# A fused attention, routed experts and dense-layer kernel: a separate one-hot chain for the first expert block, other store queue, one more block in float32r parts, new planner priorities

## The chip, the cores and the metric

One NeuronCore of one Trainium2 chip runs the whole kernel in one launch. The metric is the device time in microseconds; below 0.3% of it two versions can't be told apart.

## The reference

Three layers follow one another. All inputs are float32, except the two dense weights, which are float64.

```
attention   q, k, v [2, 8, 768, 64]; each query sees 4 sink keys and its last 128 keys; softmax; a @ v
            -> x [1536 tokens, 512]
experts     do_compute = x @ w_skip > 0;  logits = x @ w_gate (8 experts);  e = argmax, g = softmax(logits)[e]
            x += g * (relu(x @ w1[e]) @ w2[e])   for tokens with do_compute;  w1 [8, 512, 1024], w2 [8, 1024, 512]
dense       h = x @ w_in [512, 2048];  g = h if h > 0 else exp(h) - 1;  out = g @ w_out [2048, 512]
```

## The kernel before

**Order.** Nothing is scheduled by hand. A planner, the class `Plan` at the head of the file, takes a list of steps (`add`), each with the engines that can do it, an estimated time, the steps it follows, the buffers it needs and a priority. It simulates the five instruction queues ("e" TensorE, "d" VectorE, "a" ScalarE, "p" GpSimd, "s" SyncE). It starts at each point the step of lowest priority number among those that can start within a small margin. The order that comes out is what each engine's queue holds, so a step that the planner put too early makes its engine wait. The table `ADJ` shifts priorities, for a whole kind of step (key -1) or one tile of it, in units of a tile; its entries "a", "d", "e", "p", "s" are the margins.

**Attention**, 12 tiles of 128 tokens with 8 heads each: loads of k, q and v (`lk`, `lq`, `lv`, SyncE's queue; k and q share four buffers), transposes of k and q (`tk`, `tq`), scores (`qk`), mask and exp, transposes of the weights (`tp`), products with v (`av`), the output copied out of PSUM (`eo`), transposed back together with the gate columns (`tx`), scaled into rows (`fx`) and gate parts (`fm`), logits summed (`lm`). The rows go to a table in DRAM (`st`). While this runs, SyncE also loads weights of the first experts.

**Gate**, in groups of 4, 4, 2 and 2 tiles (`gate`): maximum, one-hot of the winning expert, rank within its expert by triangular and all-ones matmuls (`rk`), product of rank and one-hot (`t8`), the token's slot, and a table of token lists (`tab`, line 688). The gate weights go to DRAM by line 701.

**First expert block.** Its input is put together in PSUM. The rows of tiles 0 to 9 come by an early gather (line 862), which needs group 2's list. They are transposed (`bx00`). Tiles 10 and 11 add their own rows by a matmul with a one-hot of the slot (`hot0`, line 876; `own`, line 881). Then ScalarE or VectorE copies the sum out (`bxe`) and the first layer starts (line 915).

**Experts.** One block of 128 tokens per expert, and a ninth block for one list that overflows: gather (line 898), transpose, layer 1 (32 products), relu, layer 2, scatter. The gather of a block follows the one before it in the planner; the first waits for all stores. Blocks in `RB` split relu's output and w2 into a rounded float32r part (`hi`, line 938) and its remainder (`lo`) and multiply in three passes; the others multiply in float32. SyncE keeps loading weights.

**Dense layers.** Float64 weights are loaded as pairs of integers, turned into float32 by integer steps on VectorE (`cv`) and split in two parts. 48 steps (three groups of 512 tokens, 16 column chunks) then run layer 1 (line 1125), elu on ScalarE and VectorE (lines 1139 to 1150), layer 2 (line 1163). The conversions of the first group's chunks run beside it.

Of the kernel before, what the change touches and what calls it, by code (L numbers as in the profile page):

```python
# [17 lines left out]
P = 128  # L18
# [23 lines left out]
    "gqm": {1: 3.1},
    "hot0": {0: 0.3, 1: 2.5},
    "lk": {-1: -1.7, 3: -0.7, 8: 1.4, 9: 1.3, 10: 0.7, 11: -0.6},
    "lq": {-1: -1.3, 6: 1.3, 9: -0.2, 10: 1.1, 11: -0.9},
    "mask": {-1: -1.2},
    "mask1": {-1: 2.3},
    "p": {-1: 16.756},
    "qk": {-1: -4.3},
    "s": {-1: 0.06},  # L50
    "spt": {-1: -1.8, 2: 1.2, 4: 3.9, 10: -2.1},
# [7 lines left out]
class Plan:  # L59
# [25 lines left out]
    def run(self, adj={}, until=None):  # L85
# [90 lines left out]
def fused_kernel(  # L176
# [35 lines left out]
    NFILL = 6  # L212
# [13 lines left out]
    RB = (1, 2, 3, 4, 5, 8)  # L226
# [53 lines left out]
    gid0 = C([P, 1], I32, "gid0")  # L280
    hot0 = [C([P, P], F32, f"hot0{i}") for i in range(GROUPS[-1])]
# [215 lines left out]
    def attention(t):  # L497
# [67 lines left out]
        for g in range(2):  # L565
            def av(e, g=g):
# [15 lines left out]
                p0 + 0.1 * g + 0.09, need=[] if g else [("O", ("o", t), 1)],  # L582
# [10 lines left out]
        evict(("eo", t), lambda: sl(oT_t, ("oT", t)), lambda: bk(("o", t)), 512, [("av", t, 1)], p0 + 0.23, [("o", t)],  # L593
              need=[("oT", ("oT", t), 2)])
# [5 lines left out]
        for g in range(2):  # L600
# [5 lines left out]
            add(("tx", t, g), {"e": 0.5}, rows, [("eo", t), "eg"], p0 + 0.24, need=[("T", ("tx", t, g), 2)], use=[("oT", t)])  # L606
# [11 lines left out]
        add(("st", t), {"s": 0.45}, lambda e: nc.sync.dma_start(out=xtab[1 + t * P:1 + (t + 1) * P, 0:DM], in_=sl(x_t_, ("x", t))), [("fx", t, 1)], p0 - 2.6,  # L618
# [15 lines left out]
    def gate(gi):  # L634
# [10 lines left out]
        p0 = t0 + n - 1 + 0.28  # L645
# [55 lines left out]
        G("st", {"s": 0.45}, lambda e: nc.sync.dma_start(out=xtab[1 + t0 * P:1 + (t0 + n) * P, DM:DG].rearrange("(g p) o -> p g o", p=P),  # L701
# [68 lines left out]
    for i in range(6):  # L770
        def fill(e, i=i):
            nc.tensor.matmul(bk(("fill", i))[:, 0:256], ones, ones.rearrange("p (o n) -> p o n", o=1).to_broadcast([P, 2, P]), start=True, stop=True)
        if i < NFILL:
            add(("fill", i), {"e": 0.12}, fill, [("av", NTILE - 1, 1)] + ([("fill", i - 1)] if i else []), 1000.0, need=[("S", ("fill", i), 1)], use=[("fill", i)])
# [77 lines left out]
    def first_block():  # L852
# [18 lines left out]
        add("bx00", {"e": 0.44}, gathered, ["early", ("av", NTILE - 1, 1)], 11.25, need=[("S", ("bx", 0), 1)])  # L871
        for i in range(nl):
            t = t0 + i

            def hot(e, i=i):
                nc.vector.scalar_tensor_tensor(out=hot0[i], in0=iota, scalar=g8["t"][:, i, 0:1], in1=goh[:, i, 0:1].to_broadcast([P, P]), op0=ALU.is_equal, op1=ALU.mult)
            add(("hot0", i), {"d": 0.26}, hot, [("g", gl, "t8")], 11.2)
# [14 lines left out]
    def block(e):  # L892
# [9 lines left out]
        add(("gather", e), {"p": 1.1}, gather, ["aend", ("ov", 8) if last else "gidx"] + ([("gather", e - 1)] if e else stores), p0 - 25, lat=3.2,  # L902
# [652 lines left out]
```

## Time and profile before

| | |
|---|---|
| time, median of 3 runs | 531.11 us (529.7 to 531.55) |
| profiled execution | 530.91 us |
| span of its instructions | 529.1 us |
| busy: TensorE, VectorE, ScalarE, GpSimd | 506.6 (96%), 345.3 (65%), 203.6 (38%), 33.4 us |
| attention ends, first expert layer starts | 117.9, 126.8 us |
| dense layers start, last matmul ends | 255.8, 521.8 us |

Times in the rows are microseconds from the start of the span. An engine carries out its queue in order; the bracket behind a row gives its idle time and the instruction that ended it. DVE is VectorE, ACT ScalarE, POOL GpSimd, PE TensorE, SPq SyncE's queue. A float32 product stands as two matmul records.

### The profile page before, as it was taken

Reading aid. Unit: us, or ns where it says so; the run is one execution under the profiler, and the core shown is the slowest. Engines: PE = TensorE matmul, PEld = TensorE weight load, DVE = VectorE, ACT = ScalarE, POOL = GpSimd, SP = SyncE. Lnnn points to the kernel's source line nnn. Section 1 sums busy time; section 2 is a strip of 40 time slices with the busy share of each in tenths; the row PEclk is TensorE's granted clock in tenths of the full one; section 3 lists DMA queues with packets and bytes.
Section 4 is the critical chain, followed back from the end, with each engine's and each line's share of the span. In section 5 each row is a group of like instructions: output and inputs, shape, how many; then the busy total and the mean of one; then the engine's idle time right before and its main releaser. Section 6 shows DMA issues by size and latency. Waiting matters only on the chain.

```text
span 529.1 us, 8427 instructions
## 1 busy us (share of the span) xinstructions
PE 506.6 (96%) x3143; PEld 418.8 (79%) x3143; DVE 345.3 (65%) x874; ACT 203.6 (38%) x455; POOL 33.4 (6%) x47
## 2 busy tenths in 40 slices
PE   8989898997899999999999999999999999999994
PEld 4778786886599999779788888888888888888883
DVE  6867786878356686798999998463444545544342
ACT  3876766763033434353566664220101112001010
POOL 2000000001212111000000000100000010000000
PEclk9999999999999999999999999999999999999998
DMA  9999999418999699467555330220000002000002
GB/s 169 274 243 317 276 294 331 118 42 284 397 347 363 233 328 312 144 196 241 160 180 158 121 120 1 79 81 0 1 0 1 0 2 79 1 0 1 0 0 86
DMA packets 73155, 79.11 MB, mean 150 GB/s; under 512 B 43089, under 2 KB 51537, under 8 KB 73106
## 3 DMA queue, kind: packets, MB, share of 16 engines
q1 hardware_dynamic: 69826, 73.29, 44.9%
q0 software_dynamic: 1520, 4.99, 2.7%
q8 instruction: 26, 0.43, 0.3%
q10 hardware_dynamic: 1760, 0.22, 0.3%
q14 instruction: 23, 0.19, 0.1%
HBM read 69.82 MB, written 8.66 MB: 148 GB/s over the span
## 4 chain that ended last, share of the span: by engine, by line
PE 88%; DMA 7%; DVE 2%; issue 1%; ACT 1%; POOL 0%; DVEq 0%; ACTq 0%
PE bank L1125 25%; PE bank L1163 25%; PE bank L915 11%; PE bank L948 6%; DMA pl<-in_k_dram 4%; PE bank L574 4%; PE bank L533 4%; PE bank L951 3%; PE bank L462 3%; PE bank L605 2%; PE bank L561 2%; PE bank L579 1%; PE bank L560 1%; DMA r<-xtab,gidx 1%; DMA pl<-xtab,gid 1%
## 5 line engine op out<-in xcount | busy, mean ns | idle before, releaser
L1163 PE MATMUL bank<-m,gt 128*128 128x512 f32 x576 | 139.2, 390 | 0.0
L1163 PEld LDWEIGHTS bank<-m,gt 128*128 128x128 f32 x576 | 107.8, 188 | 22.2
L1125 PE MATMUL bank<-xTa,m 128*128 128x512 f32 x384 | 97.9, 390 | 0.6 <-DVE xTa L1067 0.6
L1143 ACT ACTIVATE re<-re 128x512 f32<-128x512 f32 x48 | 30.3, 632 | 156.7 <-DVE re L1141 156.3
L1125 PEld LDWEIGHTS bank<-xTa,m 128*128 128x128 f32 x384 | 72.0, 188 | 16.3 <-DVE xTa L1067 0.9
L1141 DVE TENSOR_SCALAR re<-bank 128x512 f32<-128x512 f32 x35 | 24.2, 692 | 74.9 <-PE bank L1125 74.9
L915 PEld LDWEIGHTS bank<-blk,pl 128*128 128x128 f32 x480 | 55.2, 192 | 2.5 <-issue 1.4
L915 PE MATMUL bank<-blk,pl 128*128 128x128 f32 x480 | 56.1, 275 | 0.7 <-ACT blk L347 0.7
L547 ACT ACTIVATE pw<-sm,rm 128x272 f32<-128x272 f32 (+2 forms) x96 | 47.1, 495 | 7.0 <-DVE rm L539 7.0
L1146 DVE SCALAR_TENSOR_TENSOR re<-re,bank 128x512 f32<-128x512 f32 x48 | 32.9, 686 | 23.9 <-ACT re L1143 23.7
L1125 PE MATMUL bank<-xTxb,m 128*128 128x512 f32 x144 | 40.4, 389 | 0.0
L539 DVE CUSTOM_DVE_ANT_0 sm<-bank,mk 128x272 f32<-128x272 f32 (+2 forms) x96 | 35.3, 407 | 6.0 <-PE bank L533 3.6
L948 PE MATMUL bank<-hl,hr 128*128 128x512 f32 (+1 forms) x168 | 36.3, 367 | 1.1 <-DVE delta L1051 1.1
L948 PEld LDWEIGHTS bank<-hl,hr 128*128 128x128 f32 x168 | 27.7, 189 | 5.5 <-DVE delta L1051 1.3
L1125 PEld LDWEIGHTS bank<-xTxb,m 128*128 128x128 f32 x144 | 27.0, 188 | 5.6
L292 DVE TENSOR_TENSOR gt<-re,gt 128x512 fp32r<-128x512 f32 x44 | 30.4, 690 | 1.0
L533 PE MATMUL bank<-kt,pl 64*128 64x272 f32 (+2 forms) x192 | 27.4, 407 | 0.0
L292 DVE TENSOR_TENSOR hl<-pl,hl 128x1024 fp32r<-128x1024 f32 x20 | 23.9, 1219 | 3.2 <-ACT hl L938 3.2
L347 ACT COPY PT<-bank 128x512 f32<-128x512 f32 (+1 forms) x40 | 20.6, 550 | 13.3 <-PE bank L561 11.0
L574 PE MATMUL bank<-PT,pl 128*64 128x128 f32 x352 | 24.5, 279 | 0.1
L1005 ACT ACTIVATE r<-raw 128x512 f32<-128x512 f32 x32 | 21.4, 677 | 8.0 <-DVE m L292 7.5
L574 PEld LDWEIGHTS bank<-PT,pl 128*64 128x64 f32 x352 | 18.7, 136 | 5.6 <-issue 2.8
(203 smaller groups left out, 653.8 us busy)
## 6 DMA issues: line engine op xcount, KB each, us to landing
pl<-in_moe_w_dram SPq DMA_DIRECT2D x62, 512.0 KB, 6.1
raw<-in_moe_w_in_dram SPq DMA_DIRECT2D x16, 512.0 KB, 4.1
raw<-in_moe_w_out_dram SPq DMA_DIRECT2D x16, 512.0 KB, 4.3
pl<-in_k_dram SPq DMA_DIRECT2D x12, 256.0 KB, 5.5
pl<-in_q_dram SPq DMA_DIRECT2D x12, 256.0 KB, 5.3
pl<-in_v_dram SPq DMA_DIRECT2D x12, 256.0 KB, 6.0
xtab<-pl SPq DMA_DIRECT2D x12, 256.0 KB, 5.1
out_dram<-raw SPq DMA_DIRECT2D x5, 512.0 KB, 3.0
```

Of the source, the lines that this page charges most:

```text
L292: CE[e].tensor_tensor(out=o, in0=a, in1=b, op=ALU.subtract)
L533: nc.tensor.matmul(o, qT[r, p, :], rhs, start=True, stop=True)
L539: nc.vector.tensor_tensor_reduce(out=sl(sm_t, ("sm", t, h))[:, 0:n], in0=bk(("s", t, h))[:, 0:n], in1=m, scale=-scale, scalar=3.0e38, op0= ...
L547: nc.scalar.activation(out=sl(pw_t, ("pw", t))[:, h, 0:n], in_=sl(sm_t, ("sm", t, h))[:, 0:n], func=ACTF.Exp, bias=rm[:, t, h:h + 1], scal ...
L574: nc.tensor.matmul(o[i * D:(i + 1) * D, p, :], vt[:, h * D:(h + 1) * D], pT[:, (0 if y else c - 2) + i, :], start=(p == 0 and (y == 1 or n ...
L915: nc.tensor.matmul(o[:, i, :], w_tile(("w", e, kk))[:, f * P:(f + 1) * P], sl(post["xT"], ("xT", e))[:, kk, :], start=(i == 0 and kk == 0) ...
L948: nc.tensor.matmul(y, h[:, a, f % 4, :], w[:, b], start=(f == 0 and j == 0), stop=(f == KF - 1 and j == 2))
L1125: nc.tensor.matmul(bk(name), w[:, a, kk, :], x[:, b], start=(kk == 0 and i == 0), stop=(kk == KD - 1 and i == 2))
L1141: nc.vector.tensor_scalar(out=r, in0=pt, scalar1=-1.0, scalar2=0.0, op0=ALU.mult, op1=ALU.max)
L1143: nc.scalar.activation(out=r, in_=r, func=ACTF.Exp, scale=-1.0)
L1146: nc.vector.scalar_tensor_tensor(out=r, in0=r, scalar=-1.0, in1=pt, op0=ALU.add, op1=ALU.max)
L1163: nc.tensor.matmul(bk(("acc", g, i)), gt[:, a, i * P:(i + 1) * P], w[:, b, :], start=(c == 0 and j == 0), stop=(c == NCH - 1 and j == 2))
```

## The change

- The planner credits 0.25 us to a TensorE step that follows a TensorE step, and `ADJ` has new values throughout.
- Ten more filler matmuls (16 for 6), of lowest priority, after the last attention matmul.
- For the first block, tiles 10 and 11 get their one-hot of expert 0 by a chain of their own, per tile: max over the logits, skip flag, column, rank by matmuls with a column, one-hot of the slot. The last tile's output copy is done in two halves, and the group before the last has a 0.6 lower priority number.
- The row stores of tiles 10 and 11 and the last gate-weight store are issued by ScalarE instead of SyncE.
- A gather no longer follows the gather before it but all stores; block 0's own gather has a later priority.
- Block 0's first layer is split in four steps. Block 6 is added to `RB`.
- Rounded copies (`hi`, step 5 of `cv`, and in the first token group steps 0 and 3 of elu) run on ScalarE alone; `hi` of block 1 waits for the index conversion.

```diff
 ADJ:  -    "qk": {-1: -4.3},   "lk": {-1: -1.7, ...},  "lq": {-1: -1.3, ...},  "p": {-1: 16.756},
       +    "qk": {-1: -20.5, ...},  "lk": {-1: -2.6, ...},  "lq": {0: -8.3, 1: -1.4, 2: -1.1},  "lv": {-1: -2.3, ...},  "p": {-1: 1.721},
...
-            o["at"] = max([self.by[a]["end"] for a in o["after"]], default=0.0)
+            o["at"] = max([self.by[a]["end"] - 0.25 * ("e" in o["eng"] and "e" in self.by[a]["eng"]) for a in o["after"]], default=0.0)
...
-    NFILL = 6
+    NFILL = 16
-    RB = (1, 2, 3, 4, 5, 8)
+    RB = (1, 2, 3, 4, 5, 6, 8)
...
+        halves_o = 2 if t == NTILE - 1 else 1
+        for i in range(halves_o):
+            w = 512 // halves_o
+            evict(("eo", t, i), lambda i=i, w=w: sl(oT_t, ("oT", t))[:, i * w:(i + 1) * w], lambda i=i, w=w: bk(("o", t))[:, i * w:(i + 1) * w], w, ...
...
-        add(("st", t), {"s": 0.45}, lambda e: nc.sync.dma_start(...
+        add(("st", t), {"a": 0.6} if last_t(t) else {"s": 0.45}, lambda e: (nc.scalar if last_t(t) else nc.sync).dma_start(...
...
-        p0 = t0 + n - 1 + 0.28
+        p0 = t0 + n - 1 + 0.28 - (0.6 if gi == len(GROUPS) - 2 else 0)
...
-        G("st", {"s": 0.45}, lambda e: nc.sync.dma_start(...
+        G("st", {"a": 0.6} if final else {"s": 0.45}, lambda e: (nc.scalar if final else nc.sync).dma_start(...
...
-        add("bx00", {"e": 0.44}, gathered, ["early", ("av", NTILE - 1, 1)], 11.25, ...
+        add("bx00", {"e": 0.44}, gathered, ["early", ("qk", NTILE - 1, 1)], 11.25, ...
...
-                nc.vector.scalar_tensor_tensor(out=hot0[i], in0=iota, scalar=g8["t"][:, i, 0:1], in1=goh[:, i, 0:1].to_broadcast([P, P]), op0=ALU.is_equal, op1=ALU.mult)
-            add(("hot0", i), {"d": 0.26}, hot, [("g", gl, "t8")], 11.2)
+            add(("f0", t), {"d": 0.24}, lambda e, i=i, lg=lg: V.tensor_reduce(out=gs0[i][:, 0:1], in_=lg(0, E), axis=AX.X, op=ALU.max), [("lm", t)], q)
+            add(("f1", t), {"d": 0.22}, lambda e, i=i, lg=lg: V.tensor_scalar(out=gs0[i][:, 1:2], in0=lg(E, E + 1), scalar1=0.0, scalar2=None, op0=ALU.is_gt), [("lm", t)], q)
+            add(("f2", t), {"d": 0.22}, lambda e, i=i, lg=lg: V.scalar_tensor_tensor(out=go0[i], in0=lg(0, 1), scalar=gs0[i][:, 0:1], in1=gs0[i][:, 1:2], op0=ALU.is_ge, op1=ALU.mult), ...
+            def rank0(e, i=i, t=t):
+                o = bk(("f3", t))[:, 0:1]
+                nc.tensor.matmul(o, ones, ohsum[:, 0:1], start=True, stop=False)
+                for x in range(i):
+                    nc.tensor.matmul(o, ones, go0[x], start=False, stop=False)
+                nc.tensor.matmul(o, utri, go0[i], start=False, stop=True)
+                nc.vector.scalar_tensor_tensor(out=hot0[i], in0=iota, scalar=bk(("f3", t))[:, 0:1], in1=go0[i].to_broadcast([P, P]), op0=ALU.is_equal, op1=ALU.mult)
...
-        ... + ([("gather", e - 1)] if e else stores), p0 - 25, lat=3.2,
+        ... + stores, (p0 if e else 36.0) - 25, lat=3.2,
...
+            if not e:
+                for h in range(2):
+                    add(("b1", e, n) if h else ("b1x", n), {"e": 1.78}, lambda eng, n=n, h=h: layer1(eng, n, (2 * h, 2 * h + 1)), ...
...
-                    add(("hi", e, i), {"a": 1.02, "d": 0.66}, ..., [("w", e, KD + i)], ...
+                    add(("hi", e, i), {"a": 1.02}, ..., [("w", e, KD + i)] + (["gidx"] if e == 1 else [("hi", e - 1 if e < 8 else 6, i)]), ...
-            add(nm(5), {"a": 0.63, "d": 0.40}, ...
+            add(nm(5), {"a": 0.63}, ...
-        add(L(0), {"a": 0.58, "d": 0.68}, ...
+        add(L(0), {"a": 0.58} if not g else {"a": 0.58, "d": 0.68}, ...
-        add(L(3), {"d": 0.37, "a": 0.63}, ...
+        add(L(3), {"a": 0.63} if not g else {"d": 0.37, "a": 0.63}, ...
```

## Rows read from the trace of the kernel before

**Rows 1.** Stages: start:end, us, busy PE, PEld, DVE, ACT, POOL; clock, DMA, GB/s

```profile
8.40:117.90 109.50, 104.46 (x1055) 84.67 (x1056) 82.42 (x393) 78.39 (x260) 2.60 (x9) 1.00 0.89 238
117.90:126.80 8.90, 4.96 (x42) 4.24 (x42) 7.13 (x36) 0.83 (x3) 1.62 (x3) 1.00 0.59 175
126.80:143.60 16.80, 14.93 (x86) 10.76 (x87) 9.20 (x29) 4.00 (x5) 3.63 (x3) 1.00 1.04 397
...
238.00:256.90 18.90, 17.26 (x138) 16.06 (x136) 16.35 (x33) 9.07 (x16) 2.46 (x2) 1.00 0.67 227
256.90:344.00 87.10, 87.05 (x392) 72.23 (x393) 73.36 (x136) 46.02 (x76) 2.59 (x2) 1.00 0.36 112
...
sum 529.10, PE 506.65 PEld 418.81 DVE 345.34 ACT 203.62 POOL 33.37; mean PE 46.06 PEld 38.07 DVE 31.39 ACT 18.51 POOL 3.03
```

**Rows 2.** Waits of TensorE: us in total, times, longest us

```profile
PE bank L462 <- DMA pl<-in_k_dram: 6.1, 6, 1.6
...
PE bank L462 <- DMA r<-xtab,gidx: 1.8, 1, 1.8
```

**Rows 3.** Timeline from 100 to 146: start us, duration us, engine, line, operation

```profile
107.83 0.17 DVE L649 TENSOR_REDUCE g_m<-lgs 128x2 f32<-128x16 f32 x1
...
118.02 0.69 DVE L347 COPY pl<-bank 128x512 f32<-128x512 f32 x1 [1.23 <-PE bank L579]
...
120.58 0.27 DVE L620 TENSOR_REDUCE lgs<-g_u 128x9 f32<-128x72 f32 x1
...
120.88 0.17 DVE L649 TENSOR_REDUCE g_m<-lgs 128x2 f32<-128x16 f32 x1
...
122.28 0.17 DVE L654 SCALAR_TENSOR_TENSOR g_oh<-lgs,g_f 128x16 f16<-128x16 f32 x1
...
122.76 0.17 DVE L665 TENSOR_TENSOR g_t<-bank,g_oh 128x16 f32<-128x16 f32 x1
...
122.93 0.41 SPq L701 DMA_DIRECT2D xtab<-gws  x1
...
124.04 2.03 PE L881 MATMUL bank<-hot,pl 128*128 128x128 f32 x16
...
124.42 0.35 DVE L876 SCALAR_TENSOR_TENSOR hot<-iota,g_t,g_oh 128x128 f32<-128x128 f32 x1
...
126.19 0.58 ACT L347 COPY blk<-bank 128x512 f32<-128x512 f32 x1 [4.62 <-PE bank L685]
...
126.83 7.41 PE L915 MATMUL bank<-blk,pl 128*128 128x128 f32 x64 [0.67 <-ACT blk L347]
...
127.65 0.17 DVE L814 CAST gidx<-tab 128x8 int32<-128x8 f32 x1
...
131.39 1.74 POOL L898 DMA_INDIRECT r<-xtab,gidx  x1 [10.39 <-DVE r L834]
```

**Rows 4.** Chain that ended last: start us, us, what

```profile
119.35 4.12 DMA pl<-xtab,gid
...
133.44 6.04 DMA r<-xtab,gidx
...
196.01 7.14 PE bank L915 x64
...
209.11 7.14 PE bank L915 x64
...
223.57 7.14 PE bank L915 x64
```

**Rows 5.** Small stores of the gate weights, line 701, four of them

```profile
DMA to landing us min/median/max: 5.8/6.7/7.7
```

**Rows 6.** DMA issues over the span: KB each, us to landing

```profile
out_dram<-raw ACTq DMA_DIRECT2D x1, 128.0 KB, 4.6
```

**Rows 7.** Instructions of VectorE from 118 to 345: busy us, mean ns, idle before

```profile
L292 DVE TENSOR_TENSOR hl<-pl,hl 128x1024 fp32r<-128x1024 f32 x20 | 23.9, 1219 | 3.2 <-ACT hl L938 3.2
...
L933 DVE SCALAR_TENSOR_TENSOR hr<-bank,hr 128x512 fp32r<-128x512 f32 x12 | 8.3, 692 | 17.1 <-ACT hr L925 17.1
```

More of the change, by code (lines that the diff above doesn't have):

```diff
@@ L280, in fused_kernel @@
     gid0 = C([P, 1], I32, "gid0")
+    go0 = [C([P, 1], F16, f"g_o0{i}") for i in range(GROUPS[-1])]
+    gs0 = [C([P, 2], F32, f"g_s0{i}") for i in range(GROUPS[-1])]
     hot0 = [C([P, P], F32, f"hot0{i}") for i in range(GROUPS[-1])]
@@ L605, in rows @@
                     nc.tensor.matmul(bk(("tx", t, g))[:, i * CW:(i + 1) * CW], sl(oT_t, ("oT", t))[:, p * P:(p + 1) * P], eg[:, p, :], start=(i == 0), stop=(i == 1))
-            add(("tx", t, g), {"e": 0.5}, rows, [("eo", t), "eg"], p0 + 0.24, need=[("T", ("tx", t, g), 2)], use=[("oT", t)])
+            add(("tx", t, g), {"e": 0.5}, rows, [("eo", t, g if t == NTILE - 1 else 0), "eg"], p0 + 0.24, need=[("T", ("tx", t, g), 2)], use=[("oT", t)])
             def part(g, lo, hi):
@@ L769, in fused_kernel @@
     add("aend", {"s": 0.0}, a_end, [("fx", t, 1) for t in range(NTILE)] + ["zst", "gc", ("lm", NTILE - 1)], 11.5, opens=opened)
[L770 removed]
+    for i in range(NFILL):
         def fill(e, i=i):
             nc.tensor.matmul(bk(("fill", i))[:, 0:256], ones, ones.rearrange("p (o n) -> p o n", o=1).to_broadcast([P, 2, P]), start=True, stop=True)
[L773 to L774 removed]
+        add(("fill", i), {"e": 0.12}, fill, [("av", NTILE - 1, 1)] + ([("fill", i - 1)] if i else []), 1000.0, need=[("S", ("fill", i), 1)], use=[("fill", i)])
     for i, (e, j) in enumerate(worder):
@@ L901, in gather @@
             )
-        add(("gather", e), {"p": 1.1}, gather, ["aend", ("ov", 8) if last else "gidx"] + ([("gather", e - 1)] if e else stores), p0 - 25, lat=3.2,
+        add(("gather", e), {"p": 1.1}, gather, ["aend", ("ov", 8) if last else "gidx"] + stores, (p0 if e else 36.0) - 25, lat=3.2,
             need=[("xg", ("xg", e), 2 if e else 1)])
@@ L909, in block, with layer1 @@
         for n in range(2):
-            def layer1(eng, n=n):
+            def layer1(eng, n=n, parts=range(4)):
                 o = bk(("h", e, n), 4)
-                for i in range(4):
+                for i in parts:
                     f = 4 * n + i
@@ L916, in layer1 @@
                                          start=(i == 0 and kk == 0), stop=(i == 3 and kk == KD - 1))
-            add(("b1", e, n), {"e": 3.55}, layer1, [("bxe", e)] + [("w", e, kk) for kk in range(KD)], p0 + n, need=[("HB", ("h", e, n), 1)],
+            if not e:
+                for h in range(2):
+                    add(("b1", e, n) if h else ("b1x", n), {"e": 1.78}, lambda eng, n=n, h=h: layer1(eng, n, (2 * h, 2 * h + 1)), [("bxe", e)] + [("w", e, kk) for kk in range(KD)], p0 + n,
+                        need=[] if h else [("HB", ("h", e, n), 1)], use=([("xT", e)] + [("w", e, kk) for kk in range(KD)]) if h else ())
+                if n:
+                    pl.by["b1x", n]["after"].append(("b1", 0, 0))
+                pl.by["b1", e, n]["after"].append(("b1x", n))
+            else:
+              add(("b1", e, n), {"e": 3.55}, layer1, [("bxe", e)] + [("w", e, kk) for kk in range(KD)], p0 + n, need=[("HB", ("h", e, n), 1)],
                 use=[("xT", e)] + [("w", e, kk) for kk in range(KD)])
@@ L937, in block @@
                     wt = lambda i=i: w_tile(("w", e, KD + i))
-                    add(("hi", e, i), {"a": 1.02, "d": 0.66}, lambda eng, key=key, wt=wt: CPY[eng](out=hl(key)[:, 0], in_=wt()), [("w", e, KD + i)], p0 - 5 + i, port=True, need=[("HL", key, 2 if last else 1)])
+                    add(("hi", e, i), {"a": 1.02}, lambda eng, key=key, wt=wt: CPY[eng](out=hl(key)[:, 0], in_=wt()), [("w", e, KD + i)] + (["gidx"] if e == 1 else [("hi", e - 1 if e < 8 else 6, i)]), p0 - 5 + i, port=True, need=[("HL", key, 2 if last else 1)])
                     add(("lo", e, i), {"d": 1.16}, lambda eng, key=key, wt=wt: sub(hl(key)[:, 1], wt(), hl(key)[:, 0].bitcast(F32), eng), [("hi", e, i)], p0 - 5 + i, port=True, use=[("w", e, KD + i)])
@@ L1012, in fused_kernel @@
                 port=True, use=[f])
-            add(nm(5), {"a": 0.63, "d": 0.40}, lambda e, a=a, c=c, w=w: CPY[e](out=place2(c)[:, w, 0, :], in_=a()), [nm(4)] + (gate_c if not w else [("cv", c, 0, 5)]), p0 + 0.5,
+            add(nm(5), {"a": 0.63}, lambda e, a=a, c=c, w=w: CPY[e](out=place2(c)[:, w, 0, :], in_=a()), [nm(4)] + (gate_c if not w else [("cv", c, 0, 5)]), p0 + 0.5,
                 port=True, use=[("a", c, w)], need=[] if w else [("PL", ("pl", c), 1)])
```

73 lines of the change are left out of this document (44 added, 29 removed), and 4 rows, old and new, of the table ADJ.

## The prediction

> **What bounds the kernel now.** I read the stages first, then TensorE's waits, then the timeline and the chain of waits around the one place where the engine stops. TensorE's records cover 506.65 of the 529.10 us span [rows 1]: the kernel is bound by matmuls, and what an edit can give is either idle time of TensorE or matmul time itself. The stages say where the idle time lies. From 256.9 us on the engine is covered without a gap (87.05 of 87.10 in the first token group) [rows 1]. Attention, 8.4 to 117.9, has 5.0 us idle. The hand-over to the experts, 117.9 to 126.8, has 3.9 us idle, and its "busy" part holds little useful work. The first expert block, 126.8 to 143.6, has 1.87. The hand-over to the last layers, 238.0 to 256.9, has 1.64 [rows 1].
>
> Two named waits stand behind this. One is 1.8 us on the rows gathered for expert block 1; six more, 6.1 us together, are on key loads in attention [rows 2]. The hand-over itself is a chain, and [rows 3] is to be read as one: output copy at 118.02, logits of tile 11 done at 120.85, gate steps, second one-hot at 124.42 to 124.77, own rows multiplied until 126.07, copy, first layer at 126.83. Beside it runs a second chain: the early gather, issued at 119.35 and 4.12 us long [rows 4], so its rows come at 123.47 and the own-row products start only at 124.04 [rows 3]. Both chains end within a microsecond of each other; shortening one alone gives little.
>
> The sum is made against the profiled execution: 530.91 us, 1.8 above its span, 0.2 below the median of 531.11.
>
> **The change part by part.**
>
> *Short one-hot chain, tile halves, earlier group 2: -3.2 us (0 to -3.7).* Now, from the end of the logits (120.58 + 0.27 = 120.85) to the end of the second one-hot (124.42 + 0.35 = 124.77) is 3.92 us [rows 3]. The new chain for tile 11 is max, compare, one-hot column, rank matmul, hot. Gate steps follow each other by 0.18 to 0.2 us (120.88 to 122.28 holds eight issues), one-hot to the step behind its matmul is 122.28 to 122.76 = 0.48, hot is 0.35 [rows 3]. That is 0.03 + 2 x 0.2 + 0.48 + 0.35 = 1.26, so 2.66 us less. The output copy in two halves lets the transpose start after half of 0.69 us [rows 3]; I take 0.28 less (0 to 0.34). Tile 10's own product can run before tile 11 is ready, so behind the last one-hot there is one product of half of 2.03 us where 124.77 to 126.07 = 1.30 us stand now [rows 3]: 0.28 less. The sum is 3.2, and the first layer starts near 123.6.
> All of it hangs on the early gather. The new chain wants its rows by about 120, some 3.5 us earlier than now. Group 2's gate started at 107.83 [rows 3], yet its token list reached GpSimd at 119.35 [rows 4], 11.5 us later. Group 3's, with first claim on VectorE, took from 120.88 to 127.65 [rows 3], 6.8 us. So the 0.6 lower priority has up to 4.7 us to win; 3.5 is within that. If nothing is won the whole 3.2 is lost, which is the other end. Ten more filler matmuls come behind everything else. The granted clock is 1.00 in these stages already [rows 1], so they can win nothing, and I put them at 0.
>
> *Last stores on ScalarE's queue, gathers freed from each other: -1.6 us (+1.2 to -1.8).* The gather of block 1 is second in line today: block 0's was issued at 131.39 [rows 3], block 1's at 133.44 with 6.04 us to land [rows 4], 139.48 in all, when TensorE had already waited its 1.8 us. The indices were ready at 127.65 + 0.17 [rows 3]. What held GpSimd to 131.39 is the last small store: issued at 122.93 [rows 3], and this line's stores take up to 7.7 us to land [rows 5], so 130.6. On ScalarE's queue I have one row, 4.6 us for 128 KB [rows 6]; with it the store lands at 122.93 + 4.6 = 127.5. With block 1's gather first, its rows come at about 128 + 6.04 = 134.1. TensorE would then be at 123.6 + 7.14 (first layer) + (14.46 - 7.14) / 2 = 3.66 (half of the rest of a plain block, both from [rows 4]) = 134.4 before the second half of layer 2. That is just in time; I take 1.6 of the 1.8.
> The Trainium skill speaks against this edit: "DMA: Bandwidth & Descriptors", section "Issuing engines are not separate DMA queues", says that DMAs started from several engines share the same 16 DMA engines and that one more issuing engine saves only issue time. By that rule the landing stays at 130.6; this is rival 1. The trace cannot settle it: no row shows a small store on ScalarE's queue among weight loads.
> ScalarE pays for three issues of some 0.4 us (the same kind on SP's queue took 0.41 [rows 3]). It has 0.83 us of work in the 8.9 us of the hand-over [rows 1]; tile 10's store falls into attention, where an eviction may sit behind it: +0 to +0.4, taken as 0.
>
> *Block 6 in float32r parts: -1.3 us (0 to -1.4).* A block with parts takes 209.11 - 196.01 = 13.10 us from first layer to first layer, block 6 without them 223.57 - 209.11 = 14.46 [rows 4]: 1.36. VectorE pays four low parts of 1.22 us and two of 0.69 [rows 7], 6.3 us, between 180 and 220. They displace weight conversions, which may run later: in the first token group VectorE has 87.1 - 73.4 = 13.7 us free [rows 1]. Copies forced onto ScalarE (46.0 us busy of 87.1 there [rows 1]) give some of it back. If that cover were gone, each microsecond too much would show as a matmul waiting in the first group.
>
> *Split first layer of block 0, ScalarE-only copies:* 0. They let list matmuls in between and keep VectorE free for the index conversion.
>
> *New priorities and the 0.25 us credit between matmul steps:* 0, bounds +9.7 and -5.3. They rewrite the order of all twelve tiles and nothing in the trace prices that. The gain is bounded by the key waits after the start-up, at most 5.0 us of idle time there [rows 1] and 6.1 with the start [rows 2]; the loss is worked out in rival 3. I take nothing, the value nearest to the rows of before, since no row speaks for either side. In the last hand-over (1.64 us idle) I also take 0, within 1 us either way.
>
> Sum: -3.2 - 1.6 - 1.3 = -6.1, so 530.9 - 6.1 = **524.8 us**.
>
> **Rivals.**
> 1. *The store lands no earlier.* Block 1's gather goes first but still at 131.4, and lands at 137.4. If its transposes stand between the halves of layer 2, TensorE waits 137.4 - 134.4 = 3.0 us where it waited 1.8: +1.2 instead of -1.6, 527.6. For it: the loads of 512 KB are issued around it as before. Against: a second queue need not wait behind them.
>    "Queues, rings and completion order" on the same page of the Trainium skill, with engines taking turns between queues, leans to the latter.
> 2. *The early gather stays late.* Group 2's list is stretched by matmuls ahead of it in order, not by VectorE alone. Then the first 3.2 us are lost: 528.0. For it: the present list waits for the last attention matmuls; against: 4.7 us of slack to win.
> 3. *Other side: attention gets slower.* New adjustments put key loads 2.6 tiles ahead of query loads in the same four buffers (they were 0.4 ahead). Waits would move from six key transposes to query transposes, on up to ten tiles. At the longest present wait, 1.6 us [rows 2], that is 16 - 6.3 = +9.7 and 534.5. The sign turns where the wait per tile passes (6.1 + 6.3) / 10 = 1.24 us. Against: the present mean is 1.0, and weights still come last in the queue.
> 4. *The same order helps:* the key waits go, 4 of the 5.0 us idle in attention: 521.
>
> **How the numbers follow.** Forecast 0.60, rivals 1 and 2 0.10 each, rival 3 0.11, rival 4 0.09. The range to hold 8 in 10 runs from rival 4's 521 to just past rival 2: 520.8 to 529.3. The forecast's own is 522.5 to 527. A measurement of this kernel tells about 0.3%, 1.6 us, from none. Faster: all but rival 3 and thin edges of 1 and 2, 0.84; same 0.06; slower 0.10.
>
> **What would show it.** Right: block 0's first layer starts 3 us earlier against the last attention matmul; the early gather is issued before 116; no wait on gathered rows before block 1; block 6 takes 13.1 us; the first token group stays covered. Wrong: TensorE waiting on query loads, a first layer that starts on the early gather, or matmuls of the first group waiting for converted weights.

## The result, and the profile after

The changed kernel takes 525.96 us (median of 12 runs, 521.99 to 528.04); the kernel before, in the same session, 530.37 us (12 runs, 529.52 to 532.29). The ratio is 0.9896, 95% interval 0.987 to 0.9921: faster by 1% (the two medians alone give 0.9917). The forecast of 524.8 us was 1.2 us low and the range held the time. The profiled execution took 522.42 us with a span of 520.7, one of the two fastest of the twelve, so its trace shows the change on a good day; the spread itself needed explaining.

The stages of the kernel after, cut where those of [rows 1] are cut (start:end, us, busy us by engine, granted clock, DMA share, GB/s):

```profile
8.40:114.90 106.50, 103.08 (x1056) 85.37 (x1057) 78.53 (x388) 83.43 (x272) 3.51 (x9) 0.97 0.93 243
114.90:121.50 6.60, 5.77 (x53) 5.04 (x53) 4.77 (x26) 1.24 (x4) 0.44 (x2) 1.00 0.75 226
121.50:136.30 14.80, 14.80 (x87) 10.91 (x88) 11.52 (x39) 4.30 (x5) 5.49 (x4) 1.00 0.96 305
...
229.20:247.50 18.30, 16.55 (x136) 15.87 (x135) 16.09 (x31) 8.10 (x14) 1.16 (x1) 1.00 0.66 218
247.50:334.60 87.10, 87.10 (x394) 72.25 (x393) 77.45 (x141) 53.06 (x90) 1.16 (x1) 1.00 0.39 122
```

From the first matmul of one stage to the first of the next, with the last matmul's end in the kernel before at 521.75 and after at 512.88, the 8.87 us went so: attention -3.00, hand-over -2.35 (8.93 to 6.58), block 0 -1.80 (16.62 to 14.82), blocks 1 to 5 together -0.13, block 6 -1.38, block 7 -0.01, hand-over to the last layers +0.30, last layers -0.50.

TensorE's waits after (us in total, times, longest), against [rows 2]: the wait on the rows of block 1 is gone, key waits fell from 6.1 us to 2.4, and the wait on a query load grew from 0.2 (not shown there) to 1.5.

```profile
PE bank L468 <- DMA pl<-in_k_dram: 2.4, 2, 1.5
PE bank L468 <- DMA pl<-in_q_dram: 1.5, 1, 1.5
PE bank L1109 <- DMA exb<-xtab: 1.2, 1, 1.2
```

The timeline of the hand-over after (start us, us, engine, line), answering [rows 3] and [rows 4]:

```profile
112.66 1.17 POOL L870 DMA_INDIRECT pl<-xtab,gid  x1 [2.44 <-DVE gid L865]
...
116.84 3.91 SPq L732 DMA_DIRECT2D exa<-in_moe_w_dram  x3
117.29 0.28 DVE L629 TENSOR_REDUCE lgs<-g_u 128x9 f32<-128x72 f32 x1
117.51 1.06 PE L906 MATMUL bank<-hot,pl 128*128 128x128 f32 x8
117.86 0.22 DVE L888 SCALAR_TENSOR_TENSOR g_o<-lgs,g_s 128x1 f16<-128x1 f32 x1
118.41 0.49 PE L781 MATMUL bank<-ones 128*128 128x256 f16 x3
118.73 0.17 PE L893 MATMUL bank<-ohsum,ones 128*128 128x1 f16 x1
119.06 0.36 DVE L901 SCALAR_TENSOR_TENSOR hot<-iota,bank,g_o 128x128 f32<-128x128 f32 x1 [0.69 <-PE bank L896]
...
119.48 1.16 PE L906 MATMUL bank<-hot,pl 128*128 128x128 f32 x8
...
120.01 0.72 ACTq L710 DMA_DIRECT2D xtab<-gws  x1
...
120.85 0.58 ACT L353 COPY blk<-bank 128x512 f32<-128x512 f32 x1 [2.43 <-PE bank L671]
...
121.48 2.05 PE L940 MATMUL bank<-blk,pl 128*128 128x128 f32 x16 [0.79 <-ACT blk L353]
...
126.43 0.17 DVE L822 CAST gidx<-tab 128x8 int32<-128x8 f32 x1
126.88 0.97 POOL L923 DMA_INDIRECT r<-xtab,gidx  x1 [9.58 <-DVE r L811]
```

The early gather is issued at 112.66, before the last attention matmul ends, where it was issued at 119.35. From the end of the logits (117.57) to the first layer (121.48) it is 3.91 us where it was 5.98 (120.85 to 126.83). A step that costs more than foretold stands in the middle: the one-hot column is ready at 118.08, but its rank matmul starts at 118.73, behind tile 10's own product and three filler matmuls in TensorE's order. Block 1's gather starts 0.28 us after its indices; in the kernel before, block 0's gather went first and waited 3.57 (131.39 less 127.82), and block 1's came behind it.

### The profile page after: what moved, and what is told of

The parts are those of the page before. It is cut to its first block, busy times and chain, and to the rows that moved or that the text cites. A ratio compares the mean times of both kernels' runs of the same rounds, so it can differ in the third digit from the quotient of the medians.

```text
span 520.7 us, 8493 instructions
## 1 busy us (share of the span) xinstructions
PE 503.3 (97%) x3166; PEld 421.7 (81%) x3166; DVE 344.5 (66%) x866; ACT 220.6 (42%) x484; POOL 30.2 (6%) x43
## 4 chain that ended last, share of the span: by engine, by line
PE 87%; DMA 5%; DVE 3%; ACT 1%; SPq 1%; issue 1%; ACTq 0%; DVEq 0%
PE bank L1196 25%; PE bank L1158 25%; PE bank L940 11%; PE bank L981 7%; PE bank L539 4%; PE bank L580 3%; PE bank L468 2%; PE bank L614 2%; PE bank L567 2%; PE bank L566 1%; DMA exb<-xtab 1%; PE bank L984 1%; PE bank L585 1%; DMA pl<-in_q_dram 1%; DMA xtab<-pl 1%; DMA xtab<-r,sidx 1%
## 5 line engine op out<-in xcount | busy, mean ns | idle before, releaser
L1174 DVE TENSOR_SCALAR re<-bank 128x512 f32<-128x512 f32 x32 | 22.1, 691 | 66.0 <-PE bank L1158 65.9
L981 PE MATMUL bank<-hl,hr 128*128 128x512 f32 (+1 forms) x192 | 42.0, 369 | 0.0
L981 PEld LDWEIGHTS bank<-hl,hr 128*128 128x128 f32 x192 | 32.1, 189 | 5.0
L298 DVE TENSOR_TENSOR gt<-re,gt 128x512 fp32r<-128x512 f32 x48 | 33.1, 689 | 1.3
L298 DVE TENSOR_TENSOR hl<-pl,hl 128x1024 fp32r<-128x1024 f32 x24 | 28.4, 1216 | 0.0
L971 ACT CAST hl<-pl 128x1024 fp32r<-128x1024 f32 x24 | 24.4, 1046 | 5.5 <-PE bank L981 5.5
L1046 ACT CAST m<-r 128x512 fp32r<-128x512 f32 x32 | 19.6, 616 | 11.6 <-DVE r L1044 11.6
L958 ACT ACTIVATE hr<-bank 128x512 fp32r<-128x512 f32 x14 | 8.4, 597 | 37.0 <-PE bank L940 37.0
```

The source lines that it names most:

```text
L298: CE[e].tensor_tensor(out=o, in0=a, in1=b, op=ALU.subtract)
L971: add(("hi", e, i), {"a": 1.02}, lambda eng, key=key, wt=wt: CPY[eng](out=hl(key)[:, 0], in_=wt()), [("w", e, KD + i)] + (["gidx"] if e == ...
L981: nc.tensor.matmul(y, h[:, a, f % 4, :], w[:, b], start=(f == 0 and j == 0), stop=(f == KF - 1 and j == 2))
L1174: nc.vector.tensor_scalar(out=r, in0=pt, scalar1=-1.0, scalar2=0.0, op0=ALU.mult, op1=ALU.max)
```

## The experiments

The stages in one table (us, read from TensorE's timeline in each kernel's profiled execution). "To block 0" runs from the end of the last attention matmul to block 0's first layer.

```
                attention  to       block   block   block   to last  last
                ends       block 0  0       1       6       layers   layers
before          117.90      8.93    16.62   13.12   14.45   17.98    265.91
after           114.90      6.58    14.82   13.09   13.07   18.28    265.41
same_again      118.76      6.49    14.82   13.07   13.07   18.41    265.40
long_chain      117.94      8.75    14.71   13.07   13.07   18.23    265.38
late_group2     115.66      6.48    17.12   13.09   13.07   17.58    265.39
sync_store      115.99      6.49    14.81   13.07   13.07   18.41    265.40
old_gather      113.97      6.49    18.97   15.45   13.07   18.29    265.40
plain6          114.38      6.49    17.51   13.09   14.59   18.00    265.71
store_first     114.19      6.63    15.65   13.09   13.07   18.37    265.40
keep_clock      115.81      6.51    17.27   13.08   13.07   18.19    265.38
new_order_only  115.58      9.99    16.48   14.96   14.45   17.99    265.75
before_again    117.00     10.31    16.31   13.09   14.45   17.98    265.89
best            116.74      5.94    15.66   13.09   13.06   18.50    265.40
```

`old_order` (experiment 7) is not in the table, because its blocks run into each other: its attention ends at 118.02, its way to block 0 takes 13.68.

**1. The changed kernel once more** (no edit).

> The changed kernel unaltered, run again: where does its spread of 522 to 528 us lie? The profiled run of 522.42 us was one of the fastest of 12; its stages were attention 114.9 us, hand-over to the first expert layer 6.6, block 0 15.0, block 6 13.1. Theory (spread lies in attention, from loads that arrive earlier or later): hand-over 6.6 +- 0.2, block 0 15.0 +- 0.2, blocks 1 to 8 equal within 0.3, and the whole difference in time to the 522.42 us run stands before the last attention matmul. Rival (spread lies in the expert blocks or behind, by gathers or a lower clock): attention 114.9 +- 0.5 and other stages longer.

Measured: 526.15 us (525.94 to 528.57), ratio 0.9899 [0.9861, 0.9936]. Every stage from the hand-over on repeats within 0.13 us; attention ends 3.9 us later. Most of it stands at one instruction. VectorE's timeline, then four windows of 2 us of the same kernel (start:end, us, busy by engine, clock, DMA):

```profile
85.81 0.42 DVE L622 TENSOR_TENSOR pl<-bank,den 128x256 f32<-128x256 f32 x1 [3.04 <-DMA xtab<-pl]
```

```profile
84.00:86.00 2.00, 0.90 (x8) 0.66 (x7) 0.19 (x1) 0.00 (x0) 0.11 (x1) 1.00 1.01 326
86.00:88.00 2.00, 1.11 (x6) 0.88 (x7) 2.00 (x12) 1.25 (x4) 0.00 (x0) 0.90 1.17 233
88.00:90.00 2.00, 2.00 (x11) 1.94 (x10) 0.84 (x7) 1.00 (x2) 0.00 (x0) 0.50 1.03 289
90.00:92.00 2.00, 2.00 (x14) 1.22 (x14) 1.48 (x7) 0.86 (x5) 0.00 (x0) 0.75 1.06 399
```

VectorE stood 3.04 us before it could write the rows of a new tile into a buffer that the store of an earlier tile was still reading. TensorE ran dry behind it (0.90 and 1.11 of 2 us busy), and then the granted clock sank, to 0.50 (1.2 GHz) in the lowest window. At the end of one group of attention matmuls the two executions of the same instruction lists were level, at 72.5 and 72.6 us; at the end of the next they stood at 90.7 and 94.6.

**2. Is it the short chain? The old long chain in its place**

```diff
-            add(("f0", t), ...)  # max
-            add(("f1", t), ...)  # compare
-            add(("f2", t), ...)  # one-hot column
-            add(("f3", t), {"e": 0.25}, rank0, ...)
-            add(("hot0", i), {"d": 0.35}, hot, [("f3", t)], q, ...)
+            add(("hot0", i), {"d": 0.26}, hot, [("g", gl, "t8")], 11.2)
```

> The changed kernel with the one-hots of tiles 10 and 11 taken from the group's gate again (both behind eight gate steps of tile 11); halves, earlier group 2 and earlier early gather stay. Five traces of the changed kernel's order give 6.5 us from the last attention matmul to the first expert layer. Theory (the short chain carries most of that stage's gain): the hand-over is 2.0 to 2.5 us longer, 8.5 to 9.0 us, near the 8.93 of before, and block 0 stays below 15.5 us. Rival (the early gather set the old hand-over and the chain hid behind it): 6.5 to 7.2 us.

Measured: 527.38 us (525.71 to 528.43), ratio 0.9922 [0.9896, 0.9948]. The hand-over is 8.75 us again, within 0.2 of before, with everything else of the change in place. TensorE waits once more for the gate's own second one-hot:

```profile
122.86 0.17 PE L667 MATMUL bank<-g_oh,utri 128*128 128x16 f16 x1 [1.09 <-DVE g_oh L663]
```

In the profiles the chain carries nearly the whole gain of the hand-over. The time moved less than 2.3 us against the changed kernel, and the intervals overlap: attention's spread is as large.

**3. Is it group 2's earlier start?**

```diff
-        p0 = t0 + n - 1 + 0.28 - (0.6 if gi == len(GROUPS) - 2 else 0)
+        p0 = t0 + n - 1 + 0.28
```

> The changed kernel without the 0.6 lower priority of gate group 2. Theory (everything hangs on the early gather's rows): the early gather is issued 3 us or more later against the last attention matmul than now (2.2 us before it), its rows come after the one-hots, and the hand-over is 8 us or more instead of 6.5. Rival (the new order and the one-hot chain alone bring group 2's list early): hand-over 6.5 to 7.0 us.

Measured: 525.53 us (523.88 to 527.73), ratio 0.9909 [0.9875, 0.9943]; hand-over 6.48. Two instructions of GpSimd and one of VectorE:

```profile
113.85 1.17 POOL L870 DMA_INDIRECT pl<-xtab,gid  x1 [3.32 <-DVE g_s L887]
...
127.09 0.17 DVE L822 CAST gidx<-tab 128x8 int32<-128x8 f32 x1
129.16 1.36 POOL L923 DMA_INDIRECT r<-xtab,gidx  x1 [11.09 <-DVE r L842]
```

Without the 0.6 the early gather is still issued 1.8 us before the last attention matmul ends (2.2 in the kernel after). The earlier start does next to nothing; what does is in experiment 7. The last two rows show something else: block 1's gather starts 1.9 us after its indices, and block 0 takes 17.12 us.

**4. Is it ScalarE's queue? The last stores back on SyncE**

```diff
-        G("st", {"a": 0.6} if final else {"s": 0.45}, lambda e: (nc.scalar if final else nc.sync).dma_start(...
+        G("st", {"s": 0.45}, lambda e: nc.sync.dma_start(...
```

The stores of the last two tiles' rows were put back in the same way.

> The changed kernel with its last two row stores and the last gate-weight store issued by SyncE again; every other queue holds the same order. Theory (the second queue is what lets block 1's gather start early): the small store lands 7 to 8 us after its issue instead of 5.2, the first gather starts at about 128 instead of 126.9 (counted with attention ending at 114.9), and TensorE waits 1 to 1.5 us for block 1's rows: block 0 lasts 16.0 to 16.5 us instead of 15.0. Rival (the rule that all queues share the same engines, so only issue time is saved): landing within 1 us of 5.2, block 0 15.0. Attention must be as in the changed kernel, since its order is the same.

Measured: 523.81 us (523.19 to 530.14), ratio 0.988 [0.9812, 0.9948]; block 0 takes 14.81 us, as in the kernel after.

```profile
118.78 2.32 SPq L732 DMA_DIRECT2D exa<-in_moe_w_dram  x3
121.20 0.41 SPq L710 DMA_DIRECT2D xtab<-gws  x1
...
127.42 0.17 DVE L822 CAST gidx<-tab 128x8 int32<-128x8 f32 x1
128.01 0.97 POOL L923 DMA_INDIRECT r<-xtab,gidx  x1 [9.62 <-DVE sidx L827]
```

The gather starts 0.42 us after its indices (127.59 to 128.01) with the store on SyncE's queue. In this profile and in the time, ScalarE's queue gives nothing that shows.

**5. Is it the order of the gathers? Chained again, block 0 first**

```diff
-        ... ["aend", ("ov", 8) if last else "gidx"] + stores, (p0 if e else 36.0) - 25, lat=3.2,
+        ... ["aend", ("ov", 8) if last else "gidx"] + ([("gather", e - 1)] if e else stores), p0 - 25, lat=3.2,
```

> The changed kernel with the gathers in the old order: block 0's own rows first, block 1's behind them. Theory: block 1's gather starts one gather later (1.3 to 2 us), its rows land at 133 to 134.5 where TensorE wants them at 132.4 (counted with attention ending at 114.9), so block 0 lasts 15.5 to 17 us instead of 15.0, unless the order moves the transposes behind layer 2, in which case it stays 15.0. Rival (the stores, not the order of gathers, set the old wait): 15.0 with a gather that waits for nothing.

Measured: 527.67 us (522.39 to 530.11), ratio 0.9918 [0.9882, 0.9953]. Block 0 takes 18.97 us and block 1 15.45, 4.15 and 2.36 more than after. TensorE waits once for the rows, as its list of waits says:

```profile
PE bank L468 <- DMA r<-xtab,gidx: 2.6, 1, 2.6
```

Not all of this is the order of the gathers. The small store landed late here, and the first gather started 1.8 us after its indices; three other kernels with a late store and the new order of gathers took 17.12 to 17.51 us for block 0. That leaves 1.5 to 1.9 of the 4.15 for the order. It isn't a clean undo either: the planner also moved both halves of block 0's second layer ahead of block 1's transposes. In time the old order costs 1.5 us against experiment 1's median on the same chip, and the intervals overlap.

**6. Block 6 in plain float32**

```diff
-    RB = (1, 2, 3, 4, 5, 6, 8)
+    RB = (1, 2, 3, 4, 5, 8)
```

The next line of the chain of copies, which names block 6, names block 5 instead.

> The changed kernel with block 6 in float32 again. Theory: block 6 lasts 14.45 us instead of 13.07 and nothing else moves by more than 0.3 us: +1.4 us in all. Rival (VectorE pays for the parts later): block 6 is 1.4 us longer, but the hand-over from block 8 to the dense layers is shorter by as much, since VectorE has 6 us less to do before it: 0 in all.

Measured: 526.67 us (526.1 to 528.44), ratio 0.9905 [0.9871, 0.9939]. Block 6 takes 14.59 us, the way to the last layers 18.00 and the last layers 265.71; in the kernel after they are 13.07, 18.28 and 265.41. So the parts give 1.52, 0.28 comes back at once (a wait of 1.2 us on rows of the last expert, shown above, which this kernel doesn't have), and 0.30 is won in the last layers. In time it is 0.5 us above experiment 1's median on the same chip, which is within the spread. But block 0 took 17.51 us here. SyncE, ScalarE, VectorE and GpSimd around it:

```profile
116.32 1.42 SPq L732 DMA_DIRECT2D exa<-in_moe_w_dram  x3
117.78 1.09 SPq L732 DMA_DIRECT2D exb<-in_moe_w_dram  x1
118.92 1.05 SPq L729 DMA_DIRECT2D exb<-in_moe_w_dram  x2
119.49 0.42 ACTq L710 DMA_DIRECT2D xtab<-gws  x1
125.81 0.17 DVE L822 CAST gidx<-tab 128x8 int32<-128x8 f32 x1
128.33 1.07 POOL L923 DMA_INDIRECT r<-xtab,gidx  x1 [11.55 <-DMA exb<-in_moe_w_dram]
```

The indices are ready at 125.98 and the gather waits until 128.33. Here five of the six 512-KB expert loads were issued before the small store, and the sixth with it (119.54). In the kernel after two were, and the third was still being issued (117.79 to 120.75); three came behind the store. The instruction lists are the same up to here; what is seen to differ is how far SyncE's queue had got in that execution.

**7. The order: the old priorities with everything else new, and the new priorities alone**

```diff
-o["at"] = max([self.by[a]["end"] - 0.25 * ("e" in o["eng"] and "e" in self.by[a]["eng"]) for a in o["after"]], default=0.0)
+o["at"] = max([self.by[a]["end"] for a in o["after"]], default=0.0)
```

with the table of adjustments of the kernel before; the second kernel is the reverse, the kernel before with the new table and the 0.25.

> The changed kernel with the priorities and the planner's step times of before: every part of the change but the new order. Theory (the new order gives nothing in the mean; attention's length of 114 to 119 us is scatter from the clock and from loads): attention as in the kernel before, 117 to 119 us, so 526 to 529 us in all with a hand-over below 7.5. Rival 1 (the new order is worth its 3 us of attention): the same attention, and the time is 3 us above the changed kernel's on the same chip. Rival 2 (the order carries the whole gain): 530 us or more.

> The kernel before with the new priorities and the 0.25 us credit alone; the hand-over's chain, the stores, the gathers and block 6 as before. Theory A (the new order's worth lies only in bringing the early gather forward for the short chain): attention ends at 114 to 119 us, the hand-over stays at 8.5 to 9.5 us, block 0 at 16 to 17.5, block 6 at 14.45, time 528 to 532. Theory B (the new order gains in attention by itself): last attention matmul at 115 or earlier, time 526 to 528. Theory C (either order only fits its own step list): planner mixes blocks or waits come up, time over 534.

> The kernel before once more, for a second profile: how far attention's end moves between two executions of the same kernel. If it moves as in the kernel after (114.0 to 118.8), the last attention matmul ends anywhere in 114 to 119 and no profile of one execution can price the new order there; if attention's spread is the new order's, it ends within 0.5 us of 117.9. The hand-over is 8.9, block 0 is 16.6, block 6 is 14.45 in either case.

Measured: with the old order 539.7 us (536.94 to 541.93), ratio 1.0167 [1.0113, 1.022], slower than before by 1.7%. TensorE's waits there, and its timeline where it stood longest:

```profile
PE bank L875 <- DMA pl<-xtab,gid: 4.0, 1, 4.0
PE bank L465 <- DMA r<-xtab,gidx: 3.4, 1, 3.4
```

```profile
119.41 1.17 POOL L867 DMA_INDIRECT pl<-xtab,gid  x1 [5.07 <-DVE gid L862]
...
125.92 1.11 PE L875 MATMUL bank<-ident,pl 128*128 128x128 f32 x4 [3.99 <-DMA pl<-xtab,gid]
```

The early gather is issued at 119.41, as before (119.35 in [rows 4]), with the 0.6 in place; its rows take 6.5 us instead of 4.12, and the short chain stands ready behind them. The planner also let the first blocks' layers run into each other. The new order alone takes 531.77 us (527.81 to 534.69), ratio 1.0031 [0.9998, 1.0065]: nothing, or a little lost. It issues the early gather at 113.88, and attention ends at 115.58, but the long gate chain still ends late: the hand-over takes 9.99 us, and block 1's indices come at 131.38, so block 1 takes 14.96. The kernel before, profiled again (531.16 us, ratio 1.0023 [0.9992, 1.0055]), ends attention at 117.00: its first layer starts at 127.31, the first time at 126.83. So the order is worth nothing by itself, and with the table of the kernel before the other parts are worth less than nothing. That table was made for the old list of steps; whether another one with the old priorities in attention would suit the new list was not tried.

**8. What stretches attention: the clock?** Six dummy matmuls behind the first key and query transposes, to keep TensorE busy where the granted clock sank in the first 20 us.

```diff
+    more = [2, 3, 1]
...
+                for _ in range(more.pop(0) if more else 0):
+                    nc.tensor.matmul(banks[7], ones, ones.rearrange(...).to_broadcast([P, 4, P]), start=True, stop=True)
```

> The changed kernel with six more all-ones matmuls put between the first transposes of attention, where TensorE idles; nothing else in any queue moves. In the changed kernel's traces the granted clock falls to half near 8 us, and from 8.4 to 20 us it is 0.56 to 0.74 in the mean (1.00 in the kernel before). Theory (the fall is what makes attention's length scatter): granted clock 1.00 from 8.4 to 20 us, attention 114 to 115 us, time below 524 us and a spread under 3 us. Rival (early attention waits on loads and masks, not on the clock): clock 1.00 and yet 114 to 119 us as before, time 522 to 528.

Measured: 525.17 us (524.48 to 527.65), ratio 0.9896 [0.9858, 0.9935]. From 8.4 to 20 us the clock was 0.85 (0.73 in the kernel after), and attention ended at 115.81. The theory fell: `plain6` had 1.00 there and ended at 114.38, `best`, with the same dummies, 1.00 and 116.74, `store_first` 0.56 and 114.19. What goes roughly with the end of attention is the waits on transfers behind 30 us (TensorE's on query or key loads, and VectorE's on row stores, from the lists of waits):

```
                waits, us                     attention ends
store_first     none                          114.19
old_gather      1.1 query                     113.97
plain6          1.2 query + 0.4 row store     114.38
after           1.5 query + 0.9 row store     114.90
late_group2     0.6 query + 0.9 row store     115.66
keep_clock      2.0 query                     115.81
sync_store      1.9 query + 1.8 row store     115.99
best            2.7 query + 0.5 key           116.74
long_chain      2.7 query                     117.94   (clock 0.52 and 0.62 for 4 us behind it)
same_again      3.0 row store                 118.76   (clock 0.50 and 0.75 for 4 us behind it)
```

**9. Is it the loads ahead of the store? Six of them moved behind it**

```diff
+        elif i < 2 * NPA + NRAW + 6:
+            after.append(("g", len(GROUPS) - 1, "gw"))
```

and the last stores on SyncE, as in experiment 4.

> The last gate store goes back to SyncE's queue, and the six expert-weight loads that stand right before it in SyncE's order are issued behind it. Theory (what lies ahead of the store sets when it lands, not the queue it is issued on): the store lands 3 to 5 us after its issue, below the 5.2 to 7.5 of the runs so far, the gather for block 1 starts within 0.6 us of its indices, TensorE does not wait for its rows, block 0 takes 14.8 us as in the changed kernel's profile and not the 17.1 to 17.5 of three other runs. Rival (queue sets it): the store lands 6 to 7.7 us after its issue as on SyncE's queue before, the gather starts 2 us or more after its indices, block 0 takes 16.6 to 17.5. Third: the loads moved behind the store come too late, and a first layer of blocks 1 to 3 waits for weights (a block over 13.3 us). Time: 523 to 526 by the theory, 526 to 528 by the rivals.

Measured: 522.32 us (521.92 to 522.78, 5 runs), ratio 0.9866 [0.9834, 0.9899].

```profile
119.44 0.38 SPq L710 DMA_DIRECT2D xtab<-gws  x1
120.00 1.41 SPq L732 DMA_DIRECT2D exa<-in_moe_w_dram  x3
...
125.77 0.17 DVE L824 CAST gidx<-tab 128x8 int32<-128x8 f32 x1
126.22 0.97 POOL L925 DMA_INDIRECT r<-xtab,gidx  x1 [9.62 <-DVE r L813]
```

The gather starts 0.28 us after its indices. The store's own landing isn't in the trace; it is at most 6.8 us (119.44 to 126.22), so the 3 to 5 us expected are not shown. Block 0 takes 15.65 and not 14.8, because TensorE waits 0.6 us on the rows. The gather is not later: it starts 5.40 us after the first layer, here and in the kernel after. But there the transposes began without a wait 5.55 us after its start (126.88 to 132.43), and here the rows took 6.3 (126.22 to 132.54). The six loads issued behind the store are under way meanwhile; that they slow the gather is likely and not shown. No layer of blocks 1 to 5 waited for them (13.07 to 13.09). All five runs lie below 522.8; of the changed kernel's twelve, two do, and none of its four in experiment 1.

**10. A candidate:** experiment 9 with six fillers in place of 16, and the dummies of experiment 8.

```diff
-    NFILL = 16
+    NFILL = 6
```

> As the kernel with the store ahead of six loads, with 6 filler matmuls in place of 16 in the last gap before block 0, and 6 dummy matmuls behind the first key transposes. If the fillers hold the rank matmul back in TensorE's queue, the time from the end of the last attention matmul to block 0's first layer falls from 6.5 to 5.7 to 6.2 us; if they only fill idle time it stays at 6.5, and if they had kept the clock it falls below 1.00 in the last stretch of attention. Block 0 at 14.8. Time 522 to 525.5; no gain over the changed kernel if the spread of attention (114 to 118.8 us) decides.

Measured: 522.59 us (522.16 to 524.52), ratio 0.9873 [0.9843, 0.9903]. The hand-over falls to 5.94 us:

```profile
119.13 0.28 DVE L634 TENSOR_REDUCE lgs<-g_u 128x9 f32<-128x72 f32 x1
...
119.70 0.22 DVE L895 SCALAR_TENSOR_TENSOR g_o<-lgs,g_s 128x1 f16<-128x1 f32 x1
...
120.03 0.17 PE L900 MATMUL bank<-ohsum,ones 128*128 128x1 f16 x1
...
122.68 0.49 PE L947 MATMUL bank<-blk,pl 128*128 128x128 f32 x2 [0.70 <-ACT blk L353]
```

The rank matmul now starts 0.11 us after the one-hot column (119.92), where it was 0.65; from the logits to the first layer it is 3.27 us against 3.91. So the fillers did stand in the way. In time it is no better than experiment 9.

## Why the prediction was right, and where its steps were not

**Short chain, halves, earlier group 2 (-3.2): -2.4 measured,** 8.93 to between 6.48 and 6.63 in eight profiles, and given back by the long chain (8.75). (The second profile of the kernel before has 10.31.) By its terms: from the last attention matmul to the logits 2.95 became 2.67, the 0.28 that the halves were to give. From the logits to the second one-hot 3.92 became 1.85 (117.57 to 119.42), 0.6 less than foretold. From there to the first layer it is 2.06 in both, so the 0.28 for tile 10's earlier product did not come: tile 11's product took 1.16 us and not half of 2.03, and the copy began 0.21 us after it (0.12 before). "Ten more filler matmuls ... I put them at 0" was the larger miss: they delay the rank matmul by part of the 0.65 us, and 6 in their place gave 0.6 back. That the early gather would decide was right, and it came in time; why was wrong. I credited the 0.6 of priority with "up to 4.7 us to win". It is the new order that does it: without the 0.6 the gather is at 113.85, with the 0.6 and the old order at 119.41.

**Stores and gathers (-1.6): -1.8 when it works, +0.5 to +0.9 when it does not.** In the kernel after and in its repeat block 0 took 14.82 us; in `late_group2`, `keep_clock` and `plain6`, whose stores and gathers are the same, 17.12, 17.27 and 17.51. The sum thus took the better case, and rival 1 (+1.2) the other, with too high a price. The step that failed is "with it the store lands at 122.93 + 4.6": I took one 128-KB store at the end of the kernel [rows 6], with three other output stores beside it and no load, for a small store among 512-KB loads. On ScalarE's queue it landed in 5.2 us (after), 7.1 (`keep_clock`), 7.5 (`old_gather`) and 7.6 (`late_group2`). The three late ones had four or five of the loads issued ahead of them, the early one two and a third in issue, which stood there for 2.96 us (2.95 in `same_again`, the other early profile; 0.47 in `plain6`). That the small store is what held the gather, and not the row stores that it follows too, its start shows: 0.76 to 0.81 us after the small store's landing in these three and in both profiles of the kernel before. The kernel before, on SyncE's queue with three ahead, shows in its second profile (KB, us to landing):

```profile
xtab<-gws SPq DMA_DIRECT2D x1, 1.0 KB, 7.6
```

So the count of loads alone doesn't give the landing: `sync_store` has three ahead too, and its gather could start 6.8 us after the store's issue, so its store landed within 6.1 (an estimate, by the same 0.76).
The Trainium skill's rule, "DMA: Bandwidth & Descriptors", section "Issuing engines are not separate DMA queues", held: the engine that issues saves issue time only, and the trace agrees (block 0 takes 14.81 us with the store on SyncE, 14.82 in the better case on ScalarE). That is rival 1's mechanism, and since the store on SyncE's queue left block 0 as short, the other queue was not needed for it. The other section that I had set against the rule, "Queues, rings and completion order", has engines take turns between queues; no run here shows that this brought the store forward.

**Block 6 (-1.3): -1.38,** with 0.30 given back on the way to the last layers. The last layers themselves gained 0.50 that I had not counted. A wait at their start, which both profiles of the kernel before have, is gone (0.4 us of it is left in `plain6`):

```profile
PE bank L1125 <- DVE xTa L1067: 0.6, 1, 0.6
```

The first token group stayed covered, 87.10 of 87.10.

**Order (0, bounds +9.7 and -5.3): 0 alone, as taken** (1.0031 [0.9998, 1.0065]). The 6.3 behind the upper bound is the 6.1 us of key waits and 0.2 us of a query wait that [rows 2] leaves out; the -5.3 has no working. But the framing failed: it is no term of a sum. Combined with the other parts it decides between -1% and +1.7%. Rivals 3 and 4 both came in part. The key waits behind 30 us are all but gone in the new order (4.4 and 2.6 us in the two profiles of before), as rival 4 had it; query waits of 0.6 to 2.7 us and row-store waits of 0.4 to 3.0 us took their place on one tile each, as rival 3 had it for the queries.

**The sum.** -2.4 for the hand-over, -0.3 for block 0 (two early profiles at -1.8 and three late ones at +0.7, an estimate), -1.1 for block 6 net, -0.5 in the last layers: -4.3, against 4.4 us between the medians. By this sum the forecast of -6.1 was 1.8 too much: block 0 was over-rated by 1.3, the hand-over by 0.8 and block 6 by 0.2, and the last layers gave 0.5 unasked. That the time came within 1.2 us is in part luck: the store was priced by a row that did not apply and came early in only two of seven profiles with it on ScalarE's queue, and the last layers helped. The fit of the sum is no proof either. It takes the hand-over from the first profile of the kernel before, and attention at nothing. The second profile has the hand-over 1.38 us longer, and attention ends at 117.90 and 117.00 in the two, against 113.97 to 118.76, on average 115.8, in the ten of the new order with the other parts. How much of the 4.4 us lies in attention is not shown. The -8.5 of the profiled execution holds 3.0 of attention's draw.

**Left open.** Why the same instruction lists (the kernel after, its repeat, `sync_store`, `plain6` and `store_first` are alike to about 2 us before the end of attention, and end it between 114.19 and 118.76) meet a late query load or row store in one execution and not in the next; the waits can be named, their cause cannot. And why all five runs of `store_first` were quick: its block 0 is 0.8 us slower than the best case of the kernel after, so attention must have been quick in all five, and only one was profiled. The gain over the changed kernel (522.32 against 525.96 us) is likely but not shown: the intervals of the two ratios overlap between 0.987 and 0.9899, and the two kernels were not run side by side.

## What to carry to other kernels

A small store on which a gather depends is better put ahead of the big loads in the order of issue than onto another engine's queue: the gather was free to start with its indices in both profiles of the one (`store_first`, `best`), in two of seven of the other (`old_order` left out, whose indices come late). The loads behind it can cost the gather something in turn (0.6 us of waiting here). Before pricing an order of instructions as a term of its own, ask which edits only pay because of it: undo it with the rest kept, and do it alone. And profile the kernel before twice: the end of one stage moved by 0.9 us between two executions (117.90 and 117.00), and the hand-over behind it by 1.38.

## What the runs showed of the hardware that was not expected

A short idle stretch of TensorE can cost twice, but need not. In `long_chain` it stood 2.7 us for a query load, and then ran at half the clock:

```profile
60.00:62.00 2.00, 0.01 (x1) 0.01 (x1) 0.20 (x2) 0.00 (x0) 0.00 (x0) 1.00 0.86 222
62.00:64.00 2.00, 2.00 (x9) 2.00 (x10) 0.00 (x0) 0.85 (x3) 0.00 (x0) 0.52 1.11 342
64.00:66.00 2.00, 2.00 (x13) 1.53 (x11) 1.24 (x5) 1.28 (x8) 0.00 (x0) 0.62 1.30 230
```

The granted clock is 0.52 and 0.62 in the 4 us behind the wait, and the stage ended 1.2 us later than in `best`, which waited as long in the same place and kept 1.00 from 60 to 80 us. Which of the two happens the runs do not tell.
